# A transformer layer's forward and backward pass: loads tied to explicit dependencies, value gradient begun inside the FFN backward, layer-norm output kept resident, first FFN gradient in 512 columns

## The chip, the core and the metric

The kernel runs on one core of a Trainium2 chip. The metric is the device time of one execution in microseconds. The kernel before takes 806.94 us, the median of three runs (806.27 to 819.85); the execution that was profiled has a span of 813.4 us.

A core has four computing engines with instruction streams of their own. TensorE (PE in the profile) multiplies matrices into PSUM, VectorE (DVE) and ScalarE (ACT) do elementwise work and empty PSUM, and GpSimd (POOL) here does little but issue transfers. SyncE (SP) only issues transfers. The engines meet at semaphores.

## The reference

One layer with pre-normalization: sliding local attention, then an FFN with GELU. It returns the output and, for a given `grad_out`, the gradients of x, wqkv, wo, w1, b1, w2 and b2. S is 2048, D 512, F 1792, with 32 heads of 16; every array is bf16.

```python
def _A_ref(x, wqkv, wo):
    H = 32; Dh = D // H
    W, dil = 8, 2
    qkv = (x @ wqkv).reshape(B, S, 3, H, Dh).transpose(2, 0, 3, 1, 4)
    ...
    idx = pos[:, None] - off[None, :]          # off = arange(W) * dil
    kg, vg = k[:, :, idx_c, :], v[:, :, idx_c, :]
    logits = jnp.einsum("bhsd,bhswd->bhsw", q, kg) * scale   # masked where idx < 0
    attn = softmax(logits)
    o = jnp.einsum("bhsw,bhswd->bhsd", attn, vg)
    return o.transpose(0, 2, 1, 3).reshape(B, S, D) @ wo

def _B_ref(x, w1, b1, w2, b2):
    return gelu(x @ w1 + b1) @ w2 + b2

h = x + _A_ref(layernorm(x), wqkv, wo)
h2 = h + _B_ref(layernorm(h), w1, b1, w2, b2)
# outputs: h2 and the vector-Jacobian product of grad_out with x, wqkv, wo, w1, b1, w2, b2
```

Each position attends to eight positions: itself and the ones 2, 4, ... 14 before it.

## The kernel before

The 2048 rows are cut into four chunks of 512 (`NC`), each of four tiles of 128 rows. Several products run per chunk, and the weight gradients run over all 16 row tiles (`NT`) at once.

**Attention** is done on VectorE. q, k and v are projected chunk by chunk (`f_qkv`, L321), copied out of PSUM by ScalarE (L323) and stored to DRAM arrays `q_r`, `k_r`, `v_r` in an order in which the eight neighbours of a row lie in the free dimension. `f_attn` loads them back as `k4` and `q4`, `dots` multiplies q by eight shifted views of k (L277, tiles `pa`), and TensorE sums the products over the head dimension with a matrix of zeros and ones (L282, `lg`). Softmax follows, and the weights go to DRAM as `at_r`. `f_o` loads them back as `a4`, and `wsum` (L292, L297) forms the weighted sum of v. `f_h` applies wo, adds x and makes the second layer norm.

**FFN forward**: `f_ffn1` computes, for each pair `f2` of the 14 blocks of F, u, its square z, a sigmoid s and g = u·s. It stores u, s and g to DRAM (`x_d`, `s_d`, `g_d`). `f_ffn2` multiplies by w2.

**FFN backward**: w2 and w1 are read transposed from DRAM by transfers that transpose (`w2T`, `w1T`). For each chunk `b1_gg` reloads u and s (`bu`, `bs`), forms the GELU's derivative `y`, multiplies it into `gout` times `w2T` (`psg`, L575 and L577), and stores the transposed result as `h1tm_d`. `b1_gx` multiplies by `w1T` (`psx`, L599) and takes the layer norm's backward. The gradient of w2 (`gw2_gen`, `psw2`, L544) needs g transposed: each of its 14 parts loads a tile `gtm` by a transposing transfer on SyncE. `b_go` turns the gradient into that of the attention output and stores it as `go_r`.

**Attention backward**: `b_ga` forms the gradient of the attention weights from `go_r` and `v_r` (tiles `pag`, `ga`, `gl`). `b_sum(c, sel)` forms the gradients of v (sel 2), k (sel 0) and q (sel 1) by weighted sums over row tiles `r4` and weights `ba`. `b_gx` multiplies them by `wqkvT` (`psy`). `gw1_gen` (L725), `gwo_gen` (L740) and `gwqkv_gen` (L751) are the weight gradients.

Generators are woven into each other by hand: `take(gen, n)` advances one by n steps, and `mix` runs one to its end with another beside it. That sets a priority for each instruction. A scheduler of the language then orders each engine's stream from these priorities and its own costs; within a stream the order is fixed when the program runs. Buffers come from pools: a tile with a tag and `bufs=n` has n buffers in rotation, and where a pool is released and another takes its place, the new tiles wait for the old ones' last readers. PSUM tiles have tags too: A, B and L have two banks each in rotation, T and U one each.

The transfers' order is that of the engine that issues them. In the kernel before the large ones are written where the tiles are made, so all weights are asked for at the start, and `woT` and `wqkvT` are asked for before the second chunk's FFN backward:

```python
woT = bm.tile([P, DC, D], BF16, name="woT")
...
sync.dma_start_transpose(out=woT[:], in_=wo_d[:, :])
...
mix(gw2, none)
sync.dma_start_transpose(out=wqkvT[:], in_=wqkv_d[:, :])
```

The second of these stands after the loop in the source, but the scheduler issues it at 340.83 us, inside the first chunk's FFN backward.

Of the kernel before, what the change touches and what calls it, by code (L numbers as in the profile page):

```python
# [10 lines left out]
P = 128  # L11
# [6 lines left out]
H = 32  # L18
DH = 16
# [16 lines left out]
def kernel(  # L36
# [59 lines left out]
    sync, pq = nc.sync, nc.gpsimd  # L96

# [105 lines left out]
    def load_rest():  # L203
        for g in range(G):
            pq.dma_start(out=wo[:, g, :], in_=_ap(A_wo, [[D, Q4], [DH * D, H], [1, D]], off=Q4 * g * D))
        pq.dma_start(out=b2row[:], in_=B_b2.rearrange("(a d) -> a d", a=1))
        pq.dma_start(out=b1r[:], in_=B_b1.rearrange("(ft p) -> ft p", p=P))
        pq.dma_start(out=w1[:], in_=B_w1.rearrange("(dc p) f -> p dc f", p=P))
        pq.dma_start(out=w2[:], in_=B_w2.rearrange("(ft p) d -> p ft d", p=P))
# [4 lines left out]
    def zero_pads(ts):  # L214
        for d_t, r0 in ts:
            m = d_t.shape[-1]
            pq.dma_start(out=_ap(d_t[:, :], [[m, PAD], [SP * m, Q4], [1, m]], off=r0 * m), in_=zv[:, :, 0:m])
# [52 lines left out]
    def dots(pool_, lg, q4, k4, i, nm):  # L270
# [9 lines left out]
        for d in range(Q4):  # L280
            for n in range(Q4):
                nc.tensor.matmul(lg[PR * n:PR * n + PR, :, :].rearrange("p i (w h) -> p i w h", w=W), lhsT=sel4[:],  # L282
                                 rhs=prs[n // 2][:, n % 2, :, :, H * d:H * d + H], start=(d == 0), stop=(d == Q4 - 1))
# [16 lines left out]

    PRA, PRB = 2, 3
# [12 lines left out]
    def f_qkv(c, sel):  # L314
        d_t, pad, eng = ((q_r, 0, sync), (k_r, PAD, sync), (v_r, PAD, pq))[sel]
        ln1T = lT[c]
        t_ = fr.tile([P, Q4, TC, P], BF16, name=f"qkv{sel}_{c}", tag="qkv", bufs=2)
# [15 lines left out]

    def f_attn(c):
        k4 = feat4(fr, k_r, PAD + CJ * c - HALO, CJ + HALO, f"k4_{c}", "k4", 1)
        q4 = feat4(fr, q_r, CJ * c, CJ, f"q4_{c}", "q4", 1)
        for i in range(TC // 2):
# [12 lines left out]
            nc.scalar.activation(out=e[:], in_=e[:], func=ACT.Exp, scale=scale)  # L350
# [7 lines left out]
    def f_o(c):  # L358
        a4 = att4(fr, at_r, CJ * c, CJ, f"a4_{c}", "a4", 1, 0)
        otm = fr.tile([P, TC, D], BF16, name=f"otm{c}", tag="qkv", bufs=2)  # L360
        for qd in range(Q4):
            v4 = row4(fr, v_r, qd, PAD + CJ * c - 2, CJ + 2, f"v4_{c}{qd}", "w4", 4, 0)
            ps = acc(f"pso{c}_{qd}")
            wsum(fr, ps, a4, v4, 0, f"o{c}_{qd}")
            nc.scalar.copy(out=otm[:, :, qd * P:(qd + 1) * P], in_=ps[:].rearrange("p (j m) -> p j m", j=TC))
# [24 lines left out]
    def f_ffn1(c):  # L390
        ln2T = l2T[c]
        gts[c] = []
        for f2 in range(FT // 2):
# [9 lines left out]
            nc.vector.tensor_tensor(out=z[:], in0=u[:], in1=u[:], op=ALU.mult)  # L403
# [39 lines left out]
    f_qkv(3, 1)  # L443
    put_w(0, nats[0])
    f_ln1(0)
    f_qkv(0, 1)
    zero_pads(((k_r, 0), (v_r, 0)))
    f_qkv(0, 0)
    put_w(2, nats[2])
    xs[1] = load_x(1)  # L450
    load_rest()
    f_qkv(3, 2)
    f_qkv(0, 2)
    f_attn(0)
    f_ln1(1)
# [3 lines left out]
    xs[2] = load_x(2)  # L459
    f_attn(1)  # L460
    f_qkv(3, 0)
    f_o(0)
    f_ln1(2)
    f_qkv(2, 1)
    f_qkv(2, 0)
    f_h(0)
# [8 lines left out]
    for dc in range(DC):  # L475
        pq.dma_start(out=wqkv_d[dc * P:(dc + 1) * P, :], in_=wqkv[:, dc, :])
    pq.dma_start(out=wo_d[:, :].rearrange("(g p) d -> p g d", p=P), in_=wo[:])
    zero_pads(((q_r, S), (go_r, S), (at_r, S), (gl_r, S)))
# [53 lines left out]
    def gw2_gen():  # L532
# [6 lines left out]
        for ft in range(FT):  # L539
            gtm = br1.tile([P, NT, P], BF16, name=f"gtm{ft}", tag="gtm", bufs=2)  # L540
            sync.dma_start_transpose(out=gtm[:], in_=g_d[ft * P:(ft + 1) * P, :])
            ps = acc(f"psw2{ft}", "A")
# [8 lines left out]
    def b1_gg(i):  # L551
# [4 lines left out]
        for f2 in range(FT // 2):  # L556
# [6 lines left out]
            nc.scalar.activation(out=y[:], in_=u[:], func=ACT.Square)  # L563
# [27 lines left out]
    def b1_gx(i):  # L591
        c = b1_order[i]
        t1s = gh1.pop(c)
        ln2 = br1.tile([P, TC, D], BF16, name=f"bln2{c}", tag="bln2", bufs=1)
        pq.dma_start(out=ln2[:], in_=pv(ln2_d[c]))
        for j in range(TC):
            ps = acc(f"psx{c}_{j}", "L")
# [4 lines left out]
            ln_bwd(ps[:], ln2[:, j, :], rstd2[:, t:t + 1], gout[c][:, j, :], gh[c][:, j, :], f"f{t}")  # L602
# [10 lines left out]
    wqkvT = bl.tile([P, NJ, D], BF16, name="wqkvT")  # L613
    gvt = [bl.tile([P, TC, D], BF16, name=f"gvt{c}") for c in range(NC)]
    sync.dma_start_transpose(out=woT[:], in_=wo_d[:, :])
# [13 lines left out]

    mix(b1_gx(0), none)  # L630
    for i in range(1, NC):
        for n, _ in enumerate(b1_gg(i)):
            take(gw2, n % 2)
        if i == NC - 1:
            mix(b_go(0), none)
        for n, _ in enumerate(b1_gx(i)):
            take(gw2, n % 2)
        if i > 1:
            mix(b_go(i - 1), none)
    mix(gw2, none)  # L640
    sync.dma_start_transpose(out=wqkvT[:], in_=wqkv_d[:, :])
# [10 lines left out]
    br1.release()  # L652
    bp = pool("bp1", 1, side="right")
    PRA, PRB, W4B = 3, 3, 5

    def b_ga(c):
        v4 = feat4(bm, v_r, PAD + CJ * c - HALO, CJ + HALO, f"bv4_{c}", "k4", 1)
        go4 = feat4(bm, go_r, CJ * c, CJ, f"go4_{c}", "q4", 1)
        gl = bp.tile([P, Q4, TC, 2 * H], BF16, name=f"gl{c}", tag="gl", bufs=1)
        for i in range(TC // 2):  # L660
            ga = ltile(f"ga{c}_{i}")
            dots(bp, ga, go4, v4, i, f"g{c}_{i}")
            g4 = ga[:].rearrange("p j (w h) -> p j w h", w=W)
            a4 = attn_v(c, i)
            pr = bp.tile([P, 2, W, H], F32, name=f"sp{c}_{i}", tag="e", bufs=2)
            nc.vector.tensor_tensor(out=pr[:], in0=g4, in1=a4, op=ALU.mult)
            rs = const.tile([P, 2, H], F32, name=f"rs{c}_{i}", tag="rs", bufs=2)
# [159 lines left out]
```

## The profile and the time before

| what | value |
|---|---|
| time, median of 3 | 806.94 us |
| span of the profiled execution | 813.4 us |
| mean granted TensorE clock | 0.914 |
| bytes moved, mean rate | 168.85 MB, 208 GB/s |
| VectorE's products for weighted sums (L292), attention backward | 96 of 1216 ns |
| VectorE's products pa and pag (L277) | 32 of 1214 ns and 32 of 1216 ns |
| matmuls of the first FFN gradient (L725), 256 columns | 448, busy 56.9 us |
| wait of TensorE for gtm, longest | 24.9 us |

The stages can be told by the lines that run. First comes attention with the projections, until the first FFN matmul at about 126 us. Then the FFN forward, with the attention of later chunks beside it, until 331 us. The FFN backward follows until 558 us, the value gradient with the gradient of w1 until 657 us, and then the wo gradient, key and query gradients and the last products until 813 us.

A busy share of a whole run is a mean over these stages, so it is read stage by stage. An engine that waits for a transfer may wait for the transfer's own time, for its turn on the issuing engine's queue, or for the buffer that it writes to.

### The profile page before, as it was taken

The page shows a single profiled execution, that of the slowest core. Times are in us where ns is not written, and L with a number is a line of the kernel's source. Part 1 is how long each engine was busy: PE and PEld are TensorE (multiplying, and loading weights), DVE is VectorE, ACT ScalarE, POOL GpSimd, SP SyncE. Part 2 cuts the span into 40 slices and gives each one's busy share as a digit, 9 for nine tenths or more (in the row PEclk, how much of TensorE's full clock was granted, in tenths as well). Part 3 has the DMA queues.
Part 4 walks back from the last instruction along what each step waited for, and adds up shares of the span by engine and source line. Part 5 has one row for each costly group of instructions (what it writes and reads, how often), then busy time and mean ns, then how long its engine had stood idle before and what let it go on. Part 6 is the DMA issues. An engine that isn't in the chain of part 4 may idle for free.

```text
span 813.4 us, 10782 instructions
## 1 busy us (share of the span) xinstructions
PE 656.7 (81%) x3906; PEld 297.5 (37%) x3906; DVE 553.9 (68%) x914; ACT 391.1 (48%) x554; POOL 238.2 (29%) x357
## 2 busy tenths in 40 slices
PE   2586498797697987843799988997599978999996
PEld 1232133232242333321344443443366633334442
DVE  5239948989567441331688977847699977995944
ACT  5343156755455453330576856754112233446663
POOL 5422123455344254320324342412322141000000
PEclk9899589989598998975989998999899979999999
DMA  7977778856736899798848695936889799974111
GB/s 195 337 261 208 216 224 247 283 168 198 242 117 206 199 272 282 207 148 93 167 121 215 156 207 146 212 81 239 304 282 325 218 362 352 315 233 154 34 33 46
DMA packets 105939, 168.85 MB, mean 208 GB/s; under 512 B 61181, under 2 KB 72798, under 8 KB 105886
## 3 DMA queue, kind: packets, MB, share of 16 engines
q1 hardware_dynamic: 71004, 75.51, 36.3%
q0 software_dynamic: 26800, 86.88, 34.3%
q10 hardware_dynamic: 8082, 5.77, 2.4%
q8 instruction: 30, 0.49, 0.2%
q14 instruction: 23, 0.19, 0.1%
HBM read 96.74 MB, written 58.28 MB: 191 GB/s over the span
## 4 chain that ended last, share of the span: by engine, by line
PE 38%; issue 17%; DVE 17%; DMA 14%; POOL 8%; ACT 5%; SPq 1%; POOLq 0%; DVEq 0%; ACTq 0%
PE psq L751 5%; PE psy L705 5%; PE psw L725 4%; PE pss L297 3%; PE ps L422 2%; PE psx L599 2%; PE psw L544 2%; PE psq L321 2%; PE pswo L740 2%; DVE pag L277 2%; DMA botm<-otm_d 2%; DVE pa L277 2%; PE psg L575 2%; DMA x_d<-u 2%; DVE pbo L292 1%
## 5 line engine op out<-in xcount | busy, mean ns | idle before, releaser
L292 DVE TENSOR_TENSOR pb<-ba,r 128x2048 bf16<-128x2048 bf16 x96 | 111.8, 1216 | 8.8 <-PE pss L297 5.5
L544 PE MATMUL psw<-gout,gtm 128*128 128x512 bf16 x224 | 53.4, 384 | 27.6 <-DMA gtm<-g_d 27.6
L422 PE MATMUL ps<-w,g 128*128 128x512 bf16 x224 | 59.8, 403 | 8.6 <-DVE g L409 6.3
L725 PE MATMUL psw<-h1tm,ln2a 128*128 128x256 bf16 x448 | 56.9, 282 | 8.5 <-DMA h1tm<-h1tm_d 6.7
L577 DVE CUSTOM_DVE_ANT_0 gh<-psg,by 128x512 bf16<-128x512 f32 x56 | 37.4, 685 | 34.7 <-PE psg L575 33.7
L575 PE MATMUL psg<-goutT,w2T 128*128 128x512 bf16 x224 | 60.6, 399 | 0.0
L321 PE MATMUL psq<-wqkv,ln1T 128*128 128x512 bf16 x192 | 50.4, 407 | 9.3 <-ACT qkv L323 8.8
L399 PE MATMUL psf<-ln2T,w 128*128 128x512 bf16 x224 | 55.3, 388 | 3.1 <-ACT u L401 3.0
L599 PE MATMUL psx<-w1T,gh 128*128 128x512 bf16 x224 | 55.0, 388 | 0.2
L277 DVE TENSOR_TENSOR pa<-q,k 128x2048 bf16<-128x2048 bf16 x32 | 37.8, 1214 | 23.7 <-DMA q<-q_r 20.7
L725 PEld LDWEIGHTS <-ln2a 128*128 128x128 bf16 x448 | 43.4, 101 | 23.9 <-issue 15.9
L705 PE MATMUL psy<-wqkvT,gT 128*128 128x512 bf16 x192 | 48.0, 390 | 3.0 <-DVE lua L529 2.4
L323 ACT CAST qkv<-psq 128x512 bf16<-128x512 f32 x48 | 27.2, 586 | 37.3 <-PE psq L321 27.5
L401 ACT ACTIVATE u<-psf,b1c 128x512 bf16<-128x512 f32 x56 | 36.7, 685 | 17.2 <-PE psf L399 8.7
L292 DVE TENSOR_TENSOR pbo<-a,v 128x2048 bf16<-128x2048 bf16 x32 | 38.3, 1213 | 9.0 <-DMA a<-at_r 6.3
L277 DVE TENSOR_TENSOR pag<-go,bv 128x2048 bf16<-128x2048 bf16 x32 | 37.3, 1216 | 7.6 <-DMA go<-go_r 7.6
L588 POOL DMA_DIRECT2D h1tm_d<-th x28 | 21.3, 762 | 70.5 <-ACT th L586 65.1
L544 PEld LDWEIGHTS <-gtm 128*128 128x128 bf16 x224 | 21.4, 98 | 54.0 <-DMA gtm<-g_d 28.6
L586 ACT COPY th<-pth 128x1024 bf16<-128x1024 bf16 x28 | 28.1, 1003 | 26.8 <-PE pth L584 25.0
L563 ACT ACTIVATE by<-bu 128x1024 bf16<-128x1024 bf16 x28 | 29.6, 1055 | 20.3 <-DVE gb1p L577 18.2
L297 PE MATMUL pss<-pb,sel 128*32 128x512 bf16 x384 | 35.3, 402 | 4.8 <-DVE pb L292 4.8
L407 ACT ACTIVATE s<-z 128x1024 bf16<-128x1024 bf16 x28 | 29.6, 1057 | 20.0 <-DMA s_d<-s 8.3
(169 smaller groups left out, 1297.4 us busy)
## 6 DMA issues: line engine op xcount, KB each, us to landing
v<-v_r SPq DMA_DIRECT2D x16, 576.0 KB, 5.1
r<-go_r SPq DMA_DIRECT2D x16, 576.0 KB, 6.9
r<-k_r SPq DMA_DIRECT2D x16, 576.0 KB, 9.6
r<-q_r SPq DMA_DIRECT2D x16, 576.0 KB, 5.5
x_d<-u POOLq DMA_DIRECT2D x28, 256.0 KB, 4.6
s_d<-s POOLq DMA_DIRECT2D x28, 256.0 KB, 3.4
g_d<-g POOLq DMA_DIRECT2D x28, 256.0 KB, 4.1
bu<-x_d POOLq DMA_DIRECT2D x28, 256.0 KB, 4.8
```

Source lines behind the costliest of these rows:

```text
L277: nc.vector.tensor_tensor(out=pr[:, a], in0=_ap(q_ap, [q_ap.ap[0], [P, 2], [0, W], [1, P]], off=a * TC * P), in1=_ap(k_ap, [k_ap.ap[0], [P ...
L292: nc.vector.tensor_tensor(out=pr[:], in0=_ap(a_ap, [a_ap.ap[0], [2 * H, CJ], [0, Q4], [1, H]], off=wh * H + (4 * H * wh if sg else 0)), in ...
L297: nc.tensor.matmul(ps[PR * n:PR * n + PR, :], lhsT=sel4[:], rhs=prs[wh][:, TC * n:TC * n + TC, :, :].rearrange("p j d h -> p (j d h)"), st ...
L321: nc.tensor.matmul(ps[:], lhsT=ln1T[:, dc, j * P:(j + 1) * P], rhs=wqkv[:, dc, sel * D:(sel + 1) * D], start=(dc == 0), stop=(dc == DC - 1))
L399: nc.tensor.matmul(ps[:], lhsT=w1[:, dc, ft * P:(ft + 1) * P], rhs=ln2T[:, dc, :], start=(dc == 0), stop=(dc == DC - 1))
L422: nc.tensor.matmul(ps[:], lhsT=gs[ft // 2][:, ft % 2, j * P:(j + 1) * P], rhs=w2[:, ft, :], start=(ft == 0), stop=False)
L544: nc.tensor.matmul(ps[:], lhsT=gtm[:, t, :], rhs=gout[t // TC][:, t % TC, :], start=(t == 0), stop=(t == NT - 1))
L575: nc.tensor.matmul(ps[:], lhsT=w2T[:, dc, ft * P:(ft + 1) * P], rhs=gT[:, dc, :], start=(dc == 0), stop=(dc == DC - 1))
L599: nc.tensor.matmul(ps[:], lhsT=t1s[ft // 2][:, ft % 2, j * P:(j + 1) * P], rhs=w1T[:, ft, :], start=(ft == 0), stop=(ft == FT - 1))
L705: nc.tensor.matmul(ps[:], lhsT=gT[sel][:, g, j * P:(j + 1) * P], rhs=wqkvT[:, sel * G + g, :], start=(n == 0), stop=(n == NJ - 1))
L725: nc.tensor.matmul(ps[:, i * 2 * P:(i + 1) * 2 * P], lhsT=ln2a[:, t // TC, t % TC, dc * P:(dc + 1) * P], rhs=tmx[:, t, :], start=(t == 0), ...
L751: nc.tensor.matmul(ps[:], lhsT=ln1a[:, t // TC, t % TC, dc * P:(dc + 1) * P], rhs=gts[sel, t // TC][:, t % TC, :], start=(t == 0), stop=(t ...
```

## The change

It has these parts:

- **Gates.** A helper, `gate`, adds a dependency between a transfer and an earlier instruction noted in `mark`, so that the transfer begins later than its own data would allow. The wo, b1 and b2 loads wait for the first softmax exponential, w2 for that of chunk 1, w1 for the first copy of the attention output of chunk 0. The copies of wqkv and wo to DRAM and the zero pads wait similarly. `woT` waits for the first step of pair 3 of chunk 1 in the FFN backward, and `wqkvT` moves from there to the value gradient (third product of the second group of the w1 gradient).
- **Start.** Some qkv tiles use other pools' buffers that are still unused, `k4` and `q4` of chunk 0 are loaded as soon as they are stored, and the order of the first calls changes. The logits' matmuls get a raised priority (`HP`).
- **Square.** The square of u in the FFN forward moves from VectorE to ScalarE.
- **Value gradient earlier.** `b_ga(0)` and `b_ga(1)` move into and right behind the FFN backward of the last chunk; part of the w2 gradient is kept to run beside them. Its PSUM tile moves from tag A to U, and psx of the last chunk from L to B.
- **Resident ln2.** `ln2a` is made once and filled as `b1_gx` loads each chunk; the w1 gradient reads it without a second load.
- **w1 gradient** in up to 512 columns: 64 matmuls of 256 columns and 192 of 512 in place of 448 of 256.
- **Pools.** The buffers of `b_sum` (`ba`, `r4`, `pb`) get a pool that outlives the change from value to key gradient, and output tiles `ow` rotate through four buffers in place of two.

```diff
+    def gate(ins, key):
+        tc.add_manual_dep(ins.ins, mark[key].ins.name,
+                          mybir.DependencyInfo(mybir.DependencyClass.Sync, mybir.DependencyReason.DATA), reason="begin later")
...
-        pq.dma_start(out=w1[:], in_=B_w1.rearrange("(dc p) f -> p dc f", p=P))
-        pq.dma_start(out=w2[:], in_=B_w2.rearrange("(ft p) d -> p ft d", p=P))
...
+        with tc.high_priority(HP):
...
-        t_ = fr.tile([P, Q4, TC, P], BF16, name=f"qkv{sel}_{c}", tag="qkv", bufs=2)
+        p_, tag, n_ = {(0, 1): (fb, "h", 2), (0, 0): (fb, "h", 2), (3, 2): (fb, "o0", 1), (0, 2): (fl, "ln2T", 2),
+                       (1, 1): (fl, "ln2T", 2)}.get((c, sel), (fr, "qkv", 2))
+        t_ = p_.tile([P, Q4, TC, P], BF16, name=f"qkv{sel}_{c}", tag=tag, bufs=n_)
...
-            nc.vector.tensor_tensor(out=z[:], in0=u[:], in1=u[:], op=ALU.mult)
+            nc.scalar.activation(out=z[:], in_=u[:], func=ACT.Square)
...
     f_qkv(0, 1)
-    zero_pads(((k_r, 0), (v_r, 0)))
+    f_k4(0)
     f_qkv(0, 0)
+    f_q4(0)
...
     f_attn(1)
-    f_qkv(3, 0)
-    f_o(0)
-    f_ln1(2)
+    gate(pq.dma_start(out=w2[:], in_=B_w2.rearrange("(ft p) d -> p ft d", p=P)), ("e", 1, 0))
     f_qkv(2, 1)
     f_qkv(2, 0)
+    f_o(0)
+    gate(pq.dma_start(out=w1[:], in_=B_w1.rearrange("(dc p) f -> p dc f", p=P)), ("o", 0, 0))
     f_h(0)
...
-            ps = acc(f"psw2{ft}", "A")
+            ps = acc(f"psw2{ft}", "U")
...
-            ps = acc(f"psx{c}_{j}", "L")
+            ps = acc(f"psx{c}_{j}", "L" if i < NC - 1 else "B")
...
     for i in range(1, NC):
         for n, _ in enumerate(b1_gg(i)):
-            take(gw2, n % 2)
+            take(gw2, 1 if n in (2, 5) else 0)
+            if n == 3 and i == 1:
+                load_T(woT, wo_d, ("y", 1, 3))
         if i == NC - 1:
             mix(b_go(0), none)
+            b_ga(0)
         for n, _ in enumerate(b1_gx(i)):
-            take(gw2, n % 2)
+            take(gw2, 1 if n == 1 else 0)
         if i > 1:
             mix(b_go(i - 1), none)
-    mix(gw2, none)
-    sync.dma_start_transpose(out=wqkvT[:], in_=wqkv_d[:, :])
+    b_ga(1)
+    mix(b_go(3), gw2)
...
+        for f0, nf in ((0, 2), (2, 4), (6, 4), (10, 4)):
+            tmx = bp.tile([P, NT, 4 * P], BF16, name=f"h1tm{f0}", tag="tmx", bufs=2)
+            pq.dma_start(out=tmx[:, :, 0:nf * P], in_=tm(h1tm_d[:, f0 * P:(f0 + nf) * P]))
...
     wg = gw1_gen()
-    b_ga(0)
-    take(wg)
-    mix(b_go(3), none)
-    b_ga(1)
     take(wg)
     for c in range(NC):
-        for _ in b_sum(c, 2):
+        for n, _ in enumerate(b_sum(c, 2)):
             take(wg)
+            if c == 2 and n == 0:
+                load_T(wqkvT, wqkv_d, ("ow1", 2, 2))
```

## The prediction

> **What bounds the kernel now.** I read the engine shares first, then TensorE's idle time by stage, then who ended its longest waits, then the queue behind the longest one. From the page, and from the windows I cut at stage borders (columns: length, then busy us and instruction count of PE, weight load, DVE, ACT, POOL; granted clock, DMA share, GB/s):
>
> ```profile
> PE 656.7 (81%) x3906; PEld 297.5 (37%) x3906; DVE 553.9 (68%) x914; ACT 391.1 (48%) x554; POOL 238.2 (29%) x357
> 0.00:126.00 126.00, 78.16 (x411) 31.86 (x412) 72.17 (x132) 53.16 (x79) 40.64 (x67) 0.88 0.78 240
> 126.00:331.00 205.00, 167.73 (x834) 65.95 (x831) 132.98 (x208) 111.12 (x150) 93.38 (x136) 0.89 0.76 222
> 331.00:408.00 77.00, 44.46 (x225) 19.89 (x225) 30.65 (x69) 27.35 (x30) 15.58 (x22) 0.80 0.93 149
> 408.00:558.00 150.00, 141.19 (x802) 67.67 (x801) 114.35 (x267) 102.39 (x136) 47.97 (x68) 0.97 0.64 156
> 558.00:657.00 99.00, 83.97 (x722) 53.43 (x721) 89.99 (x92) 21.03 (x35) 29.97 (x47) 0.95 0.88 294
> 657.00:720.00 63.00, 54.98 (x371) 19.49 (x370) 55.01 (x49) 23.24 (x37) 10.16 (x17) 0.89 0.99 338
> 720.00:813.40 93.40, 86.18 (x555) 39.24 (x553) 58.74 (x102) 52.77 (x88) 0.54 (x1) 1.00 0.27 83
> ```
>
> TensorE has most of the work, and it is the bound only where it is fed: 720 to 813 (92% busy) and 408 to 558 (94%). Elsewhere it idles: 48 us before the first FFN matmul, 37 us in the FFN forward, 33 us at the head of the FFN backward, 15 us in the value-gradient stage (558 to 657, where VectorE's 90 of 99 us lead), 8 us before the wo gradient. That is 141 of the 157 idle us, so the gain is in gaps, not in work. The longest gaps, from the waits and the timeline (start, length, engine, operation, [idle before <- releaser]):
>
> ```profile
> PE psw L544 <- DMA gtm<-g_d: 27.6, 2, 24.9
> 340.83 13.00 SPq L641 DMA_TRANSPOSE wqkvT<-wqkv_d  x1
> 379.34 1.89 PE L544 MATMUL psw<-gout,gtm 128*128 128x512 bf16 x4 [24.87 <-DMA gtm<-g_d]
> 36.90 1.07 ACT L323 CAST qkv<-psq 128x512 bf16<-128x512 f32 x2 [6.47 <-DMA k_r<-qkv]
> 54.18 4.63 DVE L277 TENSOR_TENSOR pa<-q,k 128x2048 bf16<-128x2048 bf16 x4 [20.69 <-DMA q<-q_r]
> 580.76 8.03 DVE L277 TENSOR_TENSOR pag<-go,bv 128x2048 bf16<-128x2048 bf16 x7 [7.55 <-DMA go<-go_r]
> ```
>
> The first three lines are one story. SyncE spends 13.0 us issuing the transpose of wqkv, which nothing needs before 666 us; the fourth gtm transpose can only be issued behind it at 353.9 and lands at 379, and TensorE stands for 24.9 us. The last three are the starts of attention and of its gradient, each behind a store and reload through DRAM.
>
> **What the Trainium skill says.** "DMA: Bandwidth & Descriptors", section Issuing engines are not separate DMA queues: transfers issued by SyncE, ScalarE and GpSimd share the same 16 engines and interleave. The trace agrees: from 340 to 382 us SyncE's queue took 73.6% of the engines for 3.14 MB, nearly all of it transposes, and GpSimd's loads bu<-x_d landed after 13.4 us against 4.8 over the run. "TensorE: Matmul & The Clock Gate", Part 2: matmuls stay in program order, only weight loads are pulled ahead. The trace agrees: psg matmuls stood behind the one psw for 24.9 us. Same page, Part 1: an idle TensorE is clocked at half speed; in 354 to 380 us the granted clock was 0.56. "ScalarE: Activation LUTs", What ACT_TABLE_LOAD costs: a switch of tables costs a load; here 1283 ns each, six in the run.
>
> **The change, part by part.**
>
> *A. Start.* The qkv tiles get other homes (L323's wait of 6.47 us for a k_r store goes), w1 and w2 (1.8 MB each, landing 8.9 to 14.4 us after about 22 us) leave the window in which k_r and q_r go out and come back, and k, q of chunk 0 are loaded as soon as stored. TensorE's order now has 136 qkv matmuls and 32 transposes before the first logits: 136 x 0.225 us (a run of 16 took 3.6 us) + 32 x 0.075 = 33 us, after the 21.6 us at which the first one runs today: 55 us. So the first logits matmul stays near its present 55.5 us, and attention of chunk 0 gains 3 us at most. But the qkv work of chunks 1 and 3 is then behind it: today psh of chunk 0 runs at 114.8 us, after 20 qkv matmuls and VectorE's last pbo product for chunk 0 at 104; it can follow that product directly. FFN matmuls start at 126 today; I take 115: minus 11, of which I give 1 back to the wait for w1. Bounds 3 and 14. **-10**. The late w1, w2 put 3.6 MB on the engines while at_r of chunk 1 goes out and back: 0 to 5, I take **+2**.
>
> *B. Squares to ScalarE.* 28 x 685 ns (L403) leave VectorE, 28 x 1055 ns (the row of L563, same operation and shape) join ScalarE; the six table loads stay six in the built order. It pays only where VectorE leads: from 120 to 200 us it is busy 71.7 of 80 us and ScalarE 52.3. Half of the squares are there: 14 x 0.685 = 9.6 us at most, 0 at least (from 200 to 331 VectorE has 65 of 131 us, nothing to gain). **-6**.
>
> *C. Transposes kept out of the FFN backward's head.* wqkvT goes to the value-gradient stage, woT behind the y of pair 3 of chunk 1. gtm of ft 3 then waits for its buffer and its own landing (6.1 us least, 8.8 median); the built order has one psw2 (16 x 0.238 = 3.8 us) and one block of psg, pth and psx (some 4 us) to run meanwhile. Of 24.9 us some 5 stay. Bounds 15 and 25. **-20**. psw2 gets one PSUM bank instead of two: 14 times the next one waits for a copy of 0.58 us, more where two stand back to back (about 5 places in the order): 0 to 14, I take **+3**.
>
> *D. FFN backward and value gradient (408 to 657, 249 us).* ga of chunks 0 and 1 moves up. One ga costs VectorE 8 x 1.216 + 2 x (0.686 + 1.02 + 0.682 + 0.683) = 15.9 us, so 32 us go from a stage where VectorE leads (90 of 99) to one where it has room (114 of 150). The w1 gradient in 512 columns: 448 x 0.127 (56.9 us) becomes 64 x 0.127 + 192 x 0.238 (53.4/224 of L544) = 53.9, 3 us less; the 192 weight loads saved (19 us) ran beside matmuls, nothing. Resident ln2a saves a second load of 4 x 512 KB. TensorE's floor for both stages is 141.2 + 84.0 - 3 = 222 us: 27 at most. But wqkvT now falls among the r4 loads: at 30.9 us of the engines for 3.14 MB (73.6% of 42 us) its 1.57 MB take 15 us. The stage moved 294 GB/s x 99 us = 29 MB; minus ln2a (2.1) and two pairs of bv and go (3.0), 24 MB at 340 GB/s (the stretch after it moves 338) is 71 us, with the transpose 86 us, where TensorE and VectorE alone need about 75. Behind wqkvT's 13 us of issue stand the r4 loads of chunk 2, for which VectorE and then in-order TensorE wait. The FFN-backward part grows by 64 ga matmuls x 0.111 = 7 us, to 154 with VectorE at 146. 154 + 86 = 240: **-9**; bounds +5 and -22.
>
> *E. Value-gradient to key-gradient border.* The row and weight buffers (ba, r4, pb) now outlive the pool change, and the built order puts key sums of chunks 0, 1 and the first psy before the wo gradient, which today waits for botm (15.3 us to landing) with 8 us of TensorE idle in the stretch: **-5**; 0 to -8. Deeper output buffers and the raised priority of the logits matmuls: nothing, since ow waits cost TensorE 1.7 us in all and pa ends the logits' waits.
>
> Sum: -10 +2 -6 -20 +3 -9 -5 = -45; 807 - 45 = **762 us**.
>
> **The rivals.** *DMA takes it back:* the deferred 5.2 MB meet the chains they now lie beside, A -3 +5, B -6, C -18 +3, D +3, E -5: -21, 786 us. For it: the DMA share is 0.88 to 0.99 in the stages that receive wqkvT; against: w1 and w2 leave a stretch that is just as full. *All gaps close:* A -14, B -10, C -25, D -22, E -8, no costs but 2: -77, 730 us. For it: VectorE's and TensorE's sums leave room for it; against: the DMA share above. *Gates stall the queues:* every gated transfer holds all that follows on its in-order queue. If w1 lands 12 us late, wqkvT's issue and landing (13 + 25 us as gtm saw it) starve the sums for 18, and psw2's single bank costs 14 x 0.95 = 13, against C's -20: +23, 830 us. For it: exactly this happened to gtm at 354; against: five r4 buffers of 2.4 us and one ga (15.9 us) stand between wqkvT and starving.
>
> **Chances.** Forecast 0.57, all gaps close 0.19, DMA takes it back 0.17, gates stall 0.07. The range 731 to 795 spans the first three cases with their unknowns; below it I leave 0.08, above it 0.11. Two per cent is 16 us (791 to 823): faster 0.84 (a third of the DMA rival falls short of it), same 0.09, slower 0.07.
>
> **What would show it.** A: first psf near 115 us. B: VectorE's share from 120 to 200 us under 0.85. C: no TensorE wait over 6 us on gtm. D: the first pag inside the FFN backward; a wait of VectorE's pb or TensorE's pss behind wqkvT of 5 to 15 us, and about 240 us from the second chunk's FFN backward to the last psw1. E: under 4 us idle before pswo. I am wrong if the head keeps a wait of 15 us or more on a transpose, or if w1 or r4 loads end the longest TensorE waits.

## The result, and the profile after

The changed kernel takes 778.14 us (median of 4 runs, 771.47 to 782.91) against 807.15 us (4 runs, 806.27 to 819.85): the ratio is 0.964, with an interval of 0.955 to 0.973. The profiled execution spans 777.8 us at a mean clock of 0.931.

The stages of the kernel after, cut at its own borders (columns as in the prediction's table), with the engines' line of its page above them:

```profile
PE 652.9 (84%) x3714; PEld 275.5 (35%) x3714; DVE 537.2 (69%) x886; ACT 415.0 (53%) x584; POOL 233.1 (30%) x350
...
0.00:124.00 124.00, 78.89 (x420) 31.84 (x420) 74.24 (x136) 54.26 (x79) 41.15 (x66) 0.85 0.77 230
124.00:321.50 197.50, 162.68 (x822) 66.51 (x821) 113.90 (x176) 135.64 (x177) 92.68 (x136) 0.89 0.79 233
321.50:380.00 58.50, 51.12 (x273) 22.99 (x273) 40.30 (x90) 34.50 (x43) 20.54 (x29) 0.97 0.75 215
380.00:508.00 128.00, 120.88 (x709) 58.09 (x708) 103.70 (x244) 91.33 (x121) 43.77 (x61) 1.00 0.63 164
508.00:624.00 116.00, 101.93 (x608) 38.40 (x610) 99.43 (x101) 25.62 (x45) 26.68 (x45) 0.94 0.84 279
```

TensorE's work hardly fell (656.7 to 652.9 us); the span fell because it idles less, 125 us in place of 157. Most of that is in the third line: at the head of the FFN backward TensorE was busy 44 of 77 us before and is busy 51 of 58.5 now, so 25 of the 32 us are saved there, at a clock of 0.97 where it had 0.80. The first line has barely moved. The last one, the value gradient, now has both engines near 100 of 116 us.

Lines that answer to the waits shown of before, from the waits and the timeline of the kernel after:

```profile
PE psw L568 <- ACT ow L571: 10.2, 8, 2.5
47.03 4.63 DVE L282 TENSOR_TENSOR pa<-q,k 128x2048 bf16<-128x2048 bf16 x4 [19.96 <-DMA q<-q_r]
85.16 1.23 DVE L282 TENSOR_TENSOR pa<-q,k 128x2048 bf16<-128x2048 bf16 x1 [4.14 <-PE lg L288]
508.51 4.62 DVE L282 TENSOR_TENSOR pag<-go,bv 128x2048 bf16<-128x2048 bf16 x4
574.63 8.07 SPq L639 DMA_TRANSPOSE wqkvT<-wqkv_d  x1
```

The 24.9 us wait for gtm is gone. What TensorE waits for in its place at the w2 gradient is the copy `ow` that empties the single PSUM bank, eight short waits. Attention starts 7 us earlier (pa at 47.03, before 54.18), but VectorE then waits for the logits. The first pag comes at 508.5, behind the last psx at 505.2, so the value gradient did not begin inside the FFN backward, whatever the title and the source's order suggest. The transpose of wqkv is issued at 574.63.

All kernels of this study, from their timelines. "Start" ends with the first psf, "FFN, head" with the layer-norm step (`jlf`) of the fourth psx of chunk 0, "rest of D" with the last psw1, and "tail" with TensorE's last matmul. Medians, ratios and intervals count the runs within 1.5% of a kernel's fastest alone, and the profiled executions of e2, e3 and e8 lie outside that band, 16, 8 and 16 us above these medians, so their stages are long. The ratios of the experiments are against executions of before made beside them, with medians of 803.9 to 804.1 us.

| kernel | median us | ratio to before, interval | start | FFN, head | rest of D | tail |
|---|---|---|---|---|---|---|
| before | 806.94 | | 126.1 | 298.7 | 232.5 | 152.3 |
| after | 778.14 | 0.964, 0.955 to 0.973 | 124.1 | 260.9 | 238.6 | 149.7 |
| e1, before with wqkvT late | 795.55 | 0.992, 0.989 to 0.995 | 127.4 | 267.6 | 244.9 | 153.5 |
| e12, before with one psw2 bank | 796.05 | 0.989, 0.986 to 0.992 | 126.2 | 278.4 | 230.5 | 152.7 |
| e2, after with two psw2 banks | 802.90 | (one run) | 124.7 | 271.2 | 269.3 | 147.6 |
| e3, after with ga inside | 785.64 | 0.978, 0.967 to 0.988 | 126.0 | 261.8 | 248.5 | 151.0 |
| e4, after, same order | 780.66 | 0.973, 0.966 to 0.980 | 124.8 | 258.9 | 237.3 | 148.3 |
| e5, after with wqkvT early | 791.52 | 0.984, 0.981 to 0.987 | 125.2 | 277.1 | 236.9 | 146.1 |
| e6, after, wqkvT in parts | 782.40 | 0.974, 0.968 to 0.980 | 125.1 | 256.1 | 238.0 | 147.6 |
| e7, after, square on VectorE | 789.13 | 0.982, 0.975 to 0.988 | 124.4 | 266.2 | 244.7 | 147.6 |
| e8, after with ga behind | 795.39 | 0.987, 0.982 to 0.991 | 124.9 | 271.7 | 256.6 | 151.6 |
| e9, after with ln2a held | 778.18 | 0.966, 0.957 to 0.975 | 125.8 | 254.6 | 244.5 | 149.8 |
| e10, after with all held | 785.90 | 0.978, 0.972 to 0.983 | 126.0 | 256.2 | 254.6 | 145.8 |
| e11, after with ln2 first | 777.90 | 0.968, 0.960 to 0.975 | 125.9 | 261.4 | 239.1 | 148.7 |

Three cautions. The profiled execution of before took 815.19 us, 8 us above its median, so its stages are somewhat long. e4 is in effect a second measurement of after (see there): the two differ by 2.5 us in the median and by 0.009 in the ratio. A difference under some 7 us between two lines is therefore not told apart here. And the w2 gradient runs in several stages: 86 of its 224 matmuls fall in "FFN, head" before and 73 after, so that about 3 us of TensorE's work (13 at 0.238 us, an estimate) went from that stage to the next.

### The profile page after: what moved, and what is told of

It is laid out like the page before. It is cut to its first block, busy times and chain, and to the rows that moved or that the text cites. A ratio compares the mean times of both kernels' runs of the same rounds, so it can differ in the third digit from the quotient of the medians.

```text
span 777.8 us, 10383 instructions
## 1 busy us (share of the span) xinstructions
PE 652.9 (84%) x3714; PEld 275.5 (35%) x3714; DVE 537.2 (69%) x886; ACT 415.0 (53%) x584; POOL 233.1 (30%) x350
## 4 chain that ended last, share of the span: by engine, by line
PE 29%; DMA 22%; issue 17%; DVE 13%; POOL 9%; ACT 8%; SPq 0%; POOLq 0%; ACTq 0%; DVEq 0%
PE psq L777 5%; PE psy L736 5%; PE psq L330 4%; DMA at_r<-attn 2%; PE psx L622 2%; DMA botm<-otm_d 2%; PE pswo L766 2%; DMA bu<-x_d 2%; DMA r<-go_r 2%; DMA w<-in_B_w_dram 2%; DMA gl_r<-gl 2%; PE ps L441 2%; DMA bs<-s_d 2%; PE pss L303 2%; DVE gh L601 2%
## 5 line engine op out<-in xcount | busy, mean ns | idle before, releaser
L751 PE MATMUL psw<-h1tm,ln2a 128*128 128x512 bf16 (+1 forms) x256 | 59.0, 363 | 7.6 <-ACT ow L754 4.4
L418 PE MATMUL psf<-ln2T,w 128*128 128x512 bf16 x224 | 58.5, 403 | 6.8 <-ACT u L420 6.2
L568 PE MATMUL psw<-gout,gtm 128*128 128x512 bf16 x224 | 54.7, 379 | 10.2 <-ACT ow L571 10.2
L441 PE MATMUL ps<-w,g 128*128 128x512 bf16 x224 | 55.0, 381 | 0.0
L330 PE MATMUL psq<-wqkv,ln1T 128*128 128x512 bf16 x192 | 47.8, 397 | 0.6 <-ACT qkv L332 0.2
L428 DVE TENSOR_TENSOR g<-u,s 128x1024 bf16<-128x1024 bf16 x28 | 19.3, 688 | 33.9 <-ACT s L426 32.2
L751 PEld LDWEIGHTS <-ln2a 128*128 128x128 bf16 x256 | 22.7, 100 | 36.5 <-issue 21.4
L418 PEld LDWEIGHTS <-w 128*128 128x128 bf16 x224 | 22.1, 101 | 36.3 <-issue 17.2
```

The lines of the kernel that those rows point to most:

```text
L330: nc.tensor.matmul(ps[:], lhsT=ln1T[:, dc, j * P:(j + 1) * P], rhs=wqkv[:, dc, sel * D:(sel + 1) * D], start=(dc == 0), stop=(dc == DC - 1))
L418: nc.tensor.matmul(ps[:], lhsT=w1[:, dc, ft * P:(ft + 1) * P], rhs=ln2T[:, dc, :], start=(dc == 0), stop=(dc == DC - 1))
L441: nc.tensor.matmul(ps[:], lhsT=gs[ft // 2][:, ft % 2, j * P:(j + 1) * P], rhs=w2[:, ft, :], start=(ft == 0), stop=False)
L568: nc.tensor.matmul(ps[:], lhsT=gtm[:, t, :], rhs=gout[t // TC][:, t % TC, :], start=(t == 0), stop=(t == NT - 1))
L751: nc.tensor.matmul(ps[:, 0:nf * P], lhsT=ln2a[:, t // TC, t % TC, dc * P:(dc + 1) * P], rhs=tmx[:, t, 0:nf * P], start=(t == 0), stop=(t = ...
```

## The experiments

**e1, the transpose alone.** The kernel before, with one transfer issued later:

```diff
-    sync.dma_start_transpose(out=wqkvT[:], in_=wqkv_d[:, :])
...
-        for _ in b_sum(c, 2):
+        for n, _ in enumerate(b_sum(c, 2)):
             take(wg)
+            if c == 2 and n == 0:
+                gate(sync.dma_start_transpose(out=wqkvT[:], in_=wqkv_d[:, :]), ("ow1", 4, 1))
```

> The kernel before with one edit: the transpose of wqkv is issued in the value gradient instead of ahead of the second chunk's FFN backward. My theory (the whole of step C comes from that one transfer in SyncE's queue): the 24.9 us wait of TensorE for gtm goes, and the time falls by 20 to 30 us, to 777 to 787 us. Rival (the head of the FFN backward is held by the full set of transposes and by the two-buffer gtm, and the transpose of wo, which stays in this kernel, takes its place): the gtm wait stays above 12 us and the time falls by 10 us or less. Second rival (what the head gains the value gradient pays back among its r4 loads): the head is 20 us or more shorter and the time falls by less than 12 us.

The time fell by 0.8% (6 to 8 us), the profiled head and FFN by 31, and the rest of D grew by 12: the second rival. TensorE's order is that of before, so the transfer alone did it. Of the 31 us, 30 lie behind the last product of the FFN forward, which makes the head as long as in the kernel after (64 us, before 94). The waits of TensorE in the head, then SyncE's queue and VectorE's wait in the value gradient:

```profile
PE psw L549 <- DMA gtm<-g_d: 5.0, 3, 2.7
```

```profile
585.09 13.74 SPq L773 DMA_TRANSPOSE wqkvT<-wqkv_d  x1
598.92 0.54 SPq L252 DMA_DIRECT2D bv<-v_r  x1
599.52 0.59 SPq L252 DMA_DIRECT2D go<-go_r  x1
...
610.11 6.91 DVE L282 TENSOR_TENSOR pag<-go,bv 128x2048 bf16<-128x2048 bf16 x6 [11.08 <-DMA go<-go_r]
```

The same 13 us of SyncE's issue that stood ahead of a gtm now stand ahead of the bv and go loads of chunk 3, and VectorE, which leads there, waits 11.1 us. In the kernel after, those two loads stand just ahead of the transpose (572.07 and 572.63 against 574.63) and the wait doesn't arise. So where a large transfer stands among others on its queue counts, and not only the stage that it is put in.

**e5, the reverse: the kernel after with the early transpose.** The diff is e1's backwards, with wqkvT's buffer in a pool that lives long enough; no other queue's order changes.

> The kernel after with the transpose of wqkv issued ahead of the second chunk's FFN backward again, as in the kernel before; the order on all other queues is unchanged. If step C's transfer is worth in this kernel what it was worth alone (the first experiment: head 26 us shorter, value gradient 9 us longer, in the time 6 us): 4 to 12 us slower than the kernel after, 782 to 790 us, with the gtm wait of 20 us or more back in the head and the stretch from the last psx to the last psw1 5 to 10 us shorter. If the whole of my -20 belongs to it: 20 us slower, about 798 us.

It took 791.5 us, 13 more than after and 11 more than e4. From its timelines of TensorE and of SyncE's queue:

```profile
372.99 1.46 PE L568 MATMUL psw<-gout,gtm 128*128 128x512 bf16 x3 [14.15 <-DMA gtm<-g_d]
```

```profile
330.59 21.18 SPq L687 DMA_TRANSPOSE wqkvT<-wqkv_d  x1
```

The wait for gtm is back (14.2 us), and so is a wait of 6.6 us for a copy of ScalarE. The FFN and head are 16 us longer and no other stage is shorter by more than 4. So its late place is worth 11 to 13 us in the kernel after, at the upper end of the 4 to 12 I had concluded from e1 or above it, and it costs the value gradient nothing there.

**e6, the transpose in three parts**, each behind a step of the third chunk's FFN backward:

```diff
-                load_T(wqkvT, wqkv_d, ("ow1", 2, 2))
...
+            if n in (1, 3, 5) and i == 2:
+                w3 = slice(n // 2 * DC, n // 2 * DC + DC)
+                gate(sync.dma_start_transpose(out=wqkvT[:, w3, :], in_=wqkv_d[:, n // 2 * D:n // 2 * D + D]), ("y", 2, n))
```

> The kernel after with the transpose of wqkv cut in three, each part issued behind a different step of the third chunk's FFN backward, where the transfer engines are 0.64 busy; the order on all other queues is unchanged. If the 15 us of the engines that wqkvT takes among the r4 loads cost the value gradient what the first experiment showed (9 us): the stretch from the last psx to the last psw1 shrinks by 5 to 9 us and the FFN backward keeps its length, 769 to 774 us. If VectorE and TensorE lead that stretch and not the transfers (TensorE 102 of 116 us, VectorE 99): within 3 us of the kernel after. If a part of 4 to 5 us of issue ahead of a gtm is enough to stall TensorE: FFN backward 5 us or more longer, and no gain.

782.4 us, and the rest of D is 238.0 us against 238.6. The second reading holds: the 1.57 MB among the r4 loads were not what the value gradient waited for.

**e12 and e2, the bank of the w2 gradient.** One line, in the kernel before and reversed in the kernel after:

```diff
-            ps = acc(f"psw2{ft}", "A")
+            ps = acc(f"psw2{ft}", "U")
```

> The kernel before with one edit: the w2 gradient's PSUM tile in tag U, one bank, as in the kernel after. Step C had this as a cost of 3 us; the second experiment, which put it back in the kernel after, was 41 us slower. If that loss came from the order that goes with the bank (in the second experiment TensorE's order has 356 matmuls in a row without one of the w2 gradient, in the kernel after 104 at most): here the order has no such stretch on either side (108 before, 85 with this edit), so the time stays within 6 us of the kernel before. If one bank is better in itself: 10 us or more faster than the kernel before. If it costs what step C said: 3 us slower.

> The kernel after with the w2 gradient's PSUM tile back in tag A (two banks in rotation) in place of U (one). My theory (TensorE's waits for the copies of ow, 10.2 us in sum in the FFN backward, are paid in full): 5 to 10 us less than the kernel after, about 770 us. Rival (the w2 gradient is only a filler there, and in A it stands in the way of the tiles that use A): no change within 3 us, or slower.

One bank made the kernel before 1.1% faster (about 9 us), although the early wqkvT was still in it. Two banks made the kernel after slower: its four runs lie between 802.9 and 823.1 us, where the slowest of the kernel after took 782.9. Neither hit my numbers, and the sign of the cost that I gave to the single bank was wrong.

The profile of e12 shows where its gain lies. SyncE's queue in e12, then the head (from the last product of the FFN forward to the end of chunk 0's psx) in before and in e12:

```profile
343.45 16.80 SPq L641 DMA_TRANSPOSE wqkvT<-wqkv_d  x1
```

```profile
330.50:424.80 94.30, 61.70 (x317) 28.29 (x317) 44.98 (x104) 40.02 (x49) 19.72 (x27) 0.82 0.82 139
332.80:404.60 71.80, 57.41 (x297) 26.11 (x303) 45.32 (x104) 39.09 (x48) 19.72 (x27) 0.95 0.85 162
```

The transpose still stands ahead of the fourth gtm, and its issue is even longer, but all that TensorE waits for gtm in this head is 2.9 us, for one weight load. It comes to the fourth gtm only after 370 us, where it stood for it from 354 on before. So the 24.9 us needed two things, the transpose in the queue and an order that asks for that gtm early: e1 took away the one, e12 the other. (Of the 22 us between the two windows, some belong to the long profile of before.)

Two windows of the FFN backward, 400 to 440 and 440 to 480 us, of e2 and then of after, show what the bank does:

```profile
400.00:440.00 40.00, 29.93 (x160) 14.09 (x159) 29.65 (x72) 24.36 (x32) 12.54 (x17) 0.87 0.49 132
440.00:480.00 40.00, 31.01 (x159) 14.71 (x157) 32.08 (x75) 25.52 (x31) 14.84 (x20) 0.83 0.45 132
```

```profile
400.00:440.00 40.00, 37.50 (x216) 17.89 (x215) 35.95 (x83) 29.37 (x38) 16.23 (x22) 1.00 0.69 166
440.00:480.00 40.00, 38.59 (x233) 18.95 (x232) 36.37 (x86) 31.72 (x42) 15.75 (x22) 1.00 0.66 183
```

TensorE runs 319 matmuls in e2 where it runs 449 in the kernel after, and the clock drops to 0.83. By the timelines, between 420 and 480 us e2 issues no matmul of the w2 gradient, and the kernel after 59; in e2's order, 80 of the 224 stand behind the last psx, where they fill nothing (47 in the kernel after). The w2 gradient is the filler that keeps TensorE busy while VectorE and ScalarE form y. With another bank the scheduler builds another order, and in e2's order the filler is missing for 356 matmuls in a row. The wait for the bank in the kernel after (10.2 us in sum) is small beside what e2 lost. That the missing filler is the whole of the loss is argued and not isolated: the head of e2's profile is longer too, with a wait of 7.3 us for a gtm, and bank and order changed together, as they did in e12, where the longest stretch without filler was about the same (108 and 85).

**e3 and e8, the value gradient's place.** In e3 the output gradient of chunk 0 is made before the last chunk's FFN backward, so that its ga can run inside:

```diff
+            if n == 2 and i == NC - 1:
+                b_ga(0)
         if i == NC - 1:
-            mix(b_go(0), none)
-            b_ga(0)
+            b_ga(1)
...
         if i > 1:
             mix(b_go(i - 1), none)
-    b_ga(1)
+        else:
+            mix(b_go(0), none)
```

In e8 both ga calls and the last `b_go` stand where the kernel before has them:

```diff
             mix(b_go(0), none)
-            b_ga(0)
...
-    b_ga(1)
-    mix(b_go(3), gw2)
+    mix(gw2, none)
...
     wg = gw1_gen()
+    b_ga(0)
     take(wg)
+    mix(b_go(3), none)
+    b_ga(1)
+    take(wg)
```

> The kernel after with the gradient of the attention output of chunk 0 made before the last chunk's FFN backward, so that the attention-weight gradients of chunks 0 and 1 are really among that chunk's psg and psx work. My theory D (32 us of VectorE's leave the stage behind the FFN backward, where VectorE leads): the FFN backward grows by 7 to 12 us, the stretch up to the last psw1 shrinks by 20 to 25 us, in sum 8 to 15 us less than the kernel after, 763 to 770 us. Rival (the FFN backward has no room: TensorE is 94% and VectorE 81% busy there): the two cancel, within 4 us of the kernel after.

> The kernel after with the attention-weight gradients of chunks 0 and 1 and the last chunk's output gradient called where the kernel before has them, behind the whole w2 gradient and beside the w1 gradient. If the early ga is what keeps D from being longer (VectorE's 32 us begin beside the last w2-gradient matmuls): the stretch from the last psx to the last psw1 is 8 to 15 us longer, 786 to 793 us. If the early ga earns little, since it starts only behind the last psx in any case: within 4 us of the kernel after.

No run of e3 came near 763 to 770 us: they lie between 780.1 and 794.2. That it is slower than after isn't shown, since the intervals of the two ratios overlap. The FFN backward from the end of chunk 0's psx to the last psx, and the stretch from there to the last psw1, in before, after and e3:

```profile
424.80:553.90 129.10, 122.02 (x693) 58.06 (x692) 96.88 (x227) 86.43 (x112) 43.83 (x62) 0.97 0.70 169
553.90:657.30 103.40, 86.70 (x749) 54.88 (x750) 93.13 (x99) 24.33 (x40) 29.97 (x47) 0.95 0.85 284
```

```profile
385.00:505.20 120.20, 113.14 (x663) 54.24 (x662) 96.96 (x227) 84.48 (x110) 42.35 (x59) 1.00 0.65 171
505.20:623.60 118.40, 104.33 (x625) 39.66 (x626) 101.20 (x105) 27.89 (x48) 26.28 (x45) 0.94 0.82 273
```

```profile
387.80:527.70 139.90, 128.71 (x767) 59.18 (x766) 124.13 (x258) 87.06 (x113) 46.65 (x67) 1.00 0.67 174
527.70:636.30 108.60, 89.70 (x524) 35.08 (x526) 73.78 (x75) 25.92 (x46) 22.67 (x37) 0.92 0.97 267
```

From before to after the FFN backward became 9 us shorter and the stretch behind it 15 longer. VectorE's work stayed where it was (97 and 93 us before, 97 and 101 in the kernel after), and 47 matmuls of the w2 gradient, about 11 us of TensorE's time, now run behind the last psx.

In e3 the work did move: VectorE has 74 us left in the second stretch, where it had 101. But that stretch is still 109 us long, with TensorE at 90 us and the transfers at 0.97. VectorE's longest wait there is for a transfer (11.7 us for ba from gl_r), and the transpose of wqkv holds SyncE's queue for 26.4 us where it took 8.1 in the kernel after:

```profile
580.27 26.36 SPq L639 DMA_TRANSPOSE wqkvT<-wqkv_d  x1
```

With VectorE relieved the transfers seem to be the next bound; I didn't isolate it. And the FFN backward of chunks 1 to 3 paid for it: it took 20 us longer, with VectorE busy 124 of 140 us. (I had expected 7 to 12 there, and 20 to 25 saved behind it, where 10 were.) TensorE was busy 113 of 120 us there already, and its work grew by 16 us: 64 ga matmuls came in, but also 28 more of the w2 gradient, which the new order puts ahead of the last psx. So e3 doesn't separate the moved ga from the filler that moved with it.

e8 is 15 to 17 us slower than e4 and after. In its profile the stretch from the last psx to the last psw1 takes 130.9 us, 12.5 more than in the kernel after, within the 8 to 15 of the first reading, and the rest of D is 18 longer. VectorE's and TensorE's waits behind the last psx in e8:

```profile
DVE sp L664 <- PE ga L288: 20.2, 6, 12.4
```

```profile
561.65 1.86 PE L749 MATMUL psw<-h1tm,ln2a 128*128 128x256 bf16 x8 [9.20 <-DMA h1tm<-h1tm_d]
563.45 0.61 PE L288 MATMUL ga<-pag,sel 128*32 128x512 bf16 x1
```

With ga called beside the w1 gradient, the in-order TensorE has w1-gradient matmuls ahead of ga's; they stand 9.2 us for h1tm to land, and VectorE waits 12.4 us for ga behind them. In the kernel after, w2-gradient matmuls stand there, whose gtm is in place, and such a wait is 1.8 us at most. (Another 11 us of e8's profile lie in "FFN, head", where TensorE's order is that of after.) So what the earlier call saves against e8 comes from what ga runs beside, and not from a start inside the FFN backward. Of the three places, that of the kernel after is better than e8's; e3's is not told apart from either.

**e7, the square back on VectorE.**

```diff
-            nc.scalar.activation(out=z[:], in_=u[:], func=ACT.Square)
+            nc.vector.tensor_tensor(out=z[:], in0=u[:], in1=u[:], op=ALU.mult)
```

> The kernel after with the FFN forward's square back on VectorE. My theory B: 3 to 8 us slower than the kernel after (781 to 786 us), the FFN forward (first psf to last product of the second FFN matmul) longer by as much. Rival (TensorE's matmuls and the transfers set the length of the FFN forward, and VectorE's new waits for ScalarE, 56 us in sum, undo what was saved): within 2 us, or faster.

789.1 us, 8 to 11 more than e4 and after, as my theory had it in the total. Where the time lies is less clear. FFN and head together are 5 to 7 us longer than in after and e4. But by the measure that the theory named, from the first psf to the last product of the second FFN matmul, e7 takes 196 us, the kernel after 197, and e4, with the same order as after, 190. Another 6 us lie in the rest of D, where TensorE's order is the same. So the total points the way of step B, and its size and place stay open. In before, e1 and e12 that stretch takes 203 to 207 us: it did become shorter, but e7 has most of that gain with the square on VectorE. What else brought it was not isolated.

**e4 and e11, the start.** The layer norm of chunk 2 is called behind `f_attn(1)` (e4), or ahead of `f_attn(0)` as shown (e11):

```diff
     xs[2] = load_x(2)
+    f_ln1(2)
     f_attn(0)
...
     f_qkv(1, 2)
-    f_ln1(2)
     f_attn(1)
```

> The kernel after with the layer norm of chunk 2, and with it the eight transposes pta, called after the attention logits of chunk 1 rather than before them. My theory for the missing gain of step A (TensorE's in-order stream puts the logits behind transposes that wait for VectorE's layer norm, and VectorE then waits for the logits): the waits of VectorE's pa for lg (3.4 and 4.1 us) go, the first FFN matmul comes 3 to 7 us earlier, the time falls by 3 to 7 us, to 771 to 775 us. Rival (the start is bound by VectorE's sums and the round trips through DRAM, so that the order within it matters little): within 2 us of the kernel after.

> The kernel after with the layer norm of chunk 2 called before the attention of chunk 0, so that its eight transposes stand elsewhere among the logits' matmuls of chunk 0 on TensorE. My theory for step A (the start gave back the 7 us by which attention began earlier because the in-order TensorE stands 8.6 us for that layer norm, and VectorE then 4.1 us for the logits): the first psf comes 3 to 7 us earlier, the time falls by as much, to 771 to 775 us. Rival (VectorE needs its 74 us of work before the first psf and its round trips through DRAM in any order): first psf within 2 us of 124, time unchanged.

In e4 the scheduler built the same order on every engine as for the kernel after, so it answers nothing and serves as a repeat. In e11 the order did change. Waits of TensorE between 40 and 124 us in the kernel after, then between 40 and 128 us in e11:

```profile
PE pta L244 <- DVE ln L235: 8.6, 1, 8.6
PE lg L288 <- DVE pa L282: 8.5, 6, 2.2
```

```profile
PE lg L288 <- DVE pa L282: 14.0, 11, 4.0
...
PE pta L244 <- DVE ln L235: 1.1, 1, 1.1
```

The wait of 8.6 us for the layer norm went, a wait for VectorE's products grew by 5.5, and the first psf stayed at 125.9. My theory for the start falls; the rival holds. In fourteen profiles of different edits the first psf lies between 124.1 and 127.4 us. What holds it wasn't isolated.

**e9 and e10, what is left in the head.** e9 holds three of the four ln2a loads back; e10 adds e6's parts and holds the first bv load.

```diff
-        pq.dma_start(out=ln2a[:, c, :, :], in_=pv(ln2_d[c]))
+        ld = pq.dma_start(out=ln2a[:, c, :, :], in_=pv(ln2_d[c]))
+        if i:
+            gate(ld, ("y", i, 3))
```

> The kernel after with the ln2a loads of chunks 1 to 3 held back, each to the fourth step of its own chunk's FFN backward; in the kernel after all four (2 MB) are issued between 327 and 341 us, ahead of a bu load on the same queue. My theory (what is left of step C's waits is the bu that ends ScalarE's wait of 3.6 us in the kernel after and of 8 to 13 us in the later runs, and it is late because ln2a and the gtm transposes are ahead of it): that wait falls under 3 us and the time by 4 to 10 us, 768 to 774 us. Rival (the gtm transposes alone fill the engines there, so that bu is late with or without ln2a): the wait stays at 4 us or more, the time within 3 us of the kernel after.

> The ninth experiment's edit, and with it the transpose of wqkv in three parts as in the sixth, and the first bv load (0.96 MB, issued at 330.6 us and not needed before 508) held to the last chunk's FFN backward. If the transfers in the head of the FFN backward are what is left to gain: 766 to 772 us, the end of the last psx at most 180 us behind the last product of the FFN forward (184 in the kernel after). Rival: as the kernel after within 3 us.

ScalarE's waits between 320 and 395 us in the kernel after, between 315 and 400 us in e9, and between 400 and 525 us in e10:

```profile
ACT by L587 <- DMA bu<-x_d: 5.6, 2, 3.6
```

```profile
ACT bu L590 <- DMA bs<-s_d: 4.1, 1, 4.1
```

```profile
ACT by L587 <- DMA bu<-x_d: 11.7, 1, 11.7
```

In e9 the wait for bu went and one of 4.1 us for bs, the next load on the same queue, took its place: 778.2 us, no change. In e10 chunk 1's ln2a is issued at 425.64, ahead of two bu loads, a little behind two parts of wqkvT (408.25); ScalarE then stands 11.7 us for bu and TensorE 10.8 behind it. FFN and head are 5 us shorter than in after, the rest of D 16 longer, and the time is 785.9 us. The wait moved from one stretch to another with the transfers; whether ln2a or the parts of wqkvT made it isn't separated, and 5 to 8 us in the total are little more than the noise. No kernel of the study is clearly faster than the kernel after.

## Why the prediction was right or wrong

The forecast of 762 us was 16 below the result, which lies in the range; the gain of 29 us was put at 45. The direction was right, and step C, the largest term, was right in mechanism. A and D failed, B's place was not confirmed, and the sum came near partly by luck. By its own steps:

**A** (-10 and +2): the stage gave -2. Attention did start earlier (first pa 7 us, where "3 us at most" was said), but by VectorE's last pbo product for chunk 0 the lead was gone (it ends at 105.4, before at 104.1), with 7.5 us of new waits for the logits in between. The first psh follows that product directly, as forecast, 9 us earlier than before. Lines of psh in before, then psh and VectorE's layer norm in the kernel after:

```profile
114.83 1.03 PE L377 MATMUL psh<-wo,oT 128*128 128x512 bf16 x4
```

```profile
105.55 1.06 PE L396 MATMUL psh<-wo,oT 128*128 128x512 bf16 x2
111.68 1.53 DVE L229 BATCH_NORM_STATS2 stb<-h 128x6 f32<-128x512 bf16 x2 [6.28 <-ACT h L398]
```

What failed is the step from there to psf. psh could be completed only behind the copies and transposes of the attention output, which the forecast priced at nothing: VectorE idles 6.28 us for `h` (as in e4, and 6.9 in e11), and h comes 5 us earlier, not 9. Then four pa products of 1.2 us, for a later chunk, stand on VectorE among the steps of the layer norm, and psf is 2 us earlier. The late w1 and w2 ended no long wait of TensorE. That is 6 us short of the forecast.

**B** (-6): VectorE's share from 120 to 200 us is 0.85 (68.08 of 80 us), not under the 0.85 that I had named. The FFN forward is 7 us shorter in the kernel after (197 in place of 204), near the forecast, but e7 has 196 with the square on VectorE. Undoing it costs 8 to 11 us in all. So the number came out, and that the square brought it isn't shown.

**C** (-20 and +3): right in mechanism. TensorE waits nowhere for gtm, moving only the transpose makes the head as short (e1), and putting only it back costs 11 to 13 us (e5) where I had said 20. What the step left out is that the order of the w2 gradient decides too whether TensorE stands there: e12 loses the wait with the transpose in place. The +3 for the single bank had the wrong sign: I priced the wait for the bank and not the order that comes with it. One bank in the kernel before gained 9 us (e12), and two in the kernel after cost at least 20 (e2), twice the bank's waits in the profile.

**D** (-9): this step failed, and it is the largest miss: the profile gives +6, 15 from the forecast. "32 us go from a stage where VectorE leads to one where it has room" was wrong twice. In the order as built ga starts behind the last psx, since `b_go(0)`, which must come first, is called only behind the last chunk's psg work. So VectorE's 32 us stayed where they were, and 11 us of TensorE's w2 gradient came to them: TensorE is busy 102 and VectorE 99 of the 116 us from 508 on, where I had priced the stretch at 86. And where ga was really moved inside (e3), the FFN backward had no such room: TensorE was 113 of 120 us busy there, and the stage grew by 20 where I had put 7, in part through w2-gradient matmuls that moved with it. My 86 us rest on transfers at 340 GB/s, the rate of another stretch; e3 shows 109 us with the transfers at 0.97 and 267 GB/s. The wait that I expected behind wqkvT didn't come in the kernel after; it came in e1.

**E** (-5): the tail gave -2.6, and TensorE waits 3.5 us for botm ahead of pswo, under the 4 that I had named.

In the profiles the steps add up to -2 (A), -38 (B and C together: -7 in the FFN forward, -30 in the head), +6 (D) and -3 (E), that is -36, of which about 7 come from the long profiled run of before. So the sum came near by luck: B and C together, 15 us better than said (8 if those 7 all lie there), made up for much of A and D. About 3 us of that and of D's +6 are only w2-gradient work that changed its stage. Undoing single parts (e5, e7, e8) costs about 11, 8 and 15 us, more together than the whole gain of 29, and e2's 20 come on top: the parts are not additive. e2, e7 and e8 also give TensorE another order.

Of the rivals, "DMA takes it back" (786) was nearer than the forecast, 8 us off against 16, but only for part of its reasons: A gained little and D cost something, as it said, while B and C gained far more than its 21. But it wasn't the deferred transfers in the kernel after that took it back (e6).

## What to carry to other kernels

A transfer that takes 13 us to issue is a wait for everything behind it on that queue: look at what stands behind it, in the stage that it leaves and in the one that it goes to, and at when the engine that needs it comes to it. A filler (here the w2 gradient) is worth what its spreading over the dependent steps is worth; before pricing a PSUM bank or a moved call, compare the order in which the filler is issued. And spare time in one engine's share of a stage is no room for moved work that another, full engine must serve too; nor is relieving the leading engine worth more than the distance to the next bound.

## What was not expected of the hardware

The issue of the same DMA transpose, 1.57 MB of wqkv, took 8.07 us of SyncE's queue in the kernel after, 6.48 in e8, 13.0 in before, 13.74 in e1, 21.18 in e5 and 26.36 in e3. What sets it was not isolated. The e5 figure fell in a stretch in which transposes, ln2a, bu and bs were all under way; but the busy share of the transfer engines during the issue was as high in the kernel after (1.14) as in e3 and e5 (1.16 each).
